# Where VectorE takes the attention's last three products out of PSUM, against the splits of the next segment's first operands

## The chip, the cores and the metric

The kernel runs on one core of a Trainium2 chip. The time is device microseconds of one execution, the median of several runs. The profile is of one execution, and its times are microseconds from the start of its span.

## The reference

The block computes a linear attention and multiplies it with a gated feed-forward network, with a residual:

```
xn = layernorm(x)                          # x: 2048 x 1024, fp32
q, k, v = split(xn @ wqkv)                 # 32 heads of 32
o = (phi(q) @ (phi(k)^T v)) / (phi(q) . sum(phi(k)) + 1e-6)
s = o @ wo                                 # the attention's output, 2048 x 1024
h = silu(xn @ w1) * (xn @ w3)              # 2048 x 3584
g = silu(h @ w2)                           # 2048 x 1024
out = x + s * g
```

## The kernel before

**Products.** Every large matrix product is done as a seven-product scheme on 2 x 2 blocks: `PRODUCTS = ["B11", "T2", "T3", "T1", "B21", "T4", "B22"]` names the right operands in the order of use, and `PARTNER` gives the left operand of each (A11, S2, S3, S1, A12, A22, S4). Each fp32 operand is split into two halves of the type fp32r, and each product of two 128 x 128 (by 512) tiles takes three matmuls: high x high (L103), high x low (L104), low x high (L105).

**Splits.** `split` (L91) makes the high half by a ScalarE cast (L95) and the low half by a VectorE subtraction (L96), which it returns. A raw operand comes by a DMA from SP's queue (L1286 for left operands, L1304 for right ones).

**The last two stages** are built from the class `Segment`. The first segment, `attention`, multiplies the scaled queries by the merged weights and gives s; after it come the feed-forward segments `layers`, which multiply h by w2 in pieces of 4 and 6 rows of 128. The first of them, `layers[0]` (two half rows, `nk` = 2), is the "second layer" of the change: the layer of operands that follows the attention. Each segment runs over `NG` = 8 blocks of 256 tokens. `right(k)` splits the seven right operands of half row k, `operands(m)` the seven left operands of block m, and `tokens(m, ...)` runs the products of block m and takes them out of PSUM.

**A block of the attention.** `tokens` uses four PSUM banks: ba (B11, then B21), bb (T2), bc (T3, then T4), bd (T1, then B22). The last three products end in c11 (a copy from ba, L1255), c21 (bc plus u) and c12 (bd plus u; both by `take`, L1199), all on VectorE. `end` then stores each c tile by a DMA from POOL's queue (L1328). The c tiles come from `small`, six buffers, which hold raw right operands of `layers[0]` too (T3 and T1 of half row 1 are loaded there ahead; B21, T4 and B22 follow as buffers come free).

**The first block of a segment** takes all seven banks at once (tiles named B11B, T2B and so on) and runs over k outside and over the products inside. The other blocks use four banks aB to dB.

**The change of segments.** Behind `run(attention, ...)` the pools of the attention's operands are closed and new ones are laid over them: `px` for the left operands (10 places of one buffer, and six raw buffers `pr`), `pw` for the right operands of half rows 1 and on. A new tile waits for the old tiles that it overlaps. Half row 0 of the right operands has been split during the attention (`first_weights`).

**Order.** Each engine works its queue strictly in the order in which it was laid down. A planner orders the queues by a simulated timeline, with the order in the code as priority. `with tc.issue_after(i)` adds an edge without a semaphore: what the block issues on the engine of instruction i comes behind i in that engine's queue. Before the change no such edge stands between the attention's evictions and the splits of `layers[0]`.

The names in the profile: `s<-as` is c11's copy, `s<-cs,us` and `s<-ds,us` the takes of c21 and c12, `XA11B<-rA11B` the split of the left operand A11 of a feed-forward segment, `B<-rB11B` and `T<-rT2B` those of right operands.

Of the kernel before, what the change touches and what calls it, by code (L numbers as in the profile page):

```python
# [22 lines left out]
def tile_linear_attention_times_swiglu(  # L23
# [27 lines left out]
    def bank(name):  # L51
        return ps.tile([P, C], F32, tag="bank", name=name)
# [38 lines left out]
    def split(pair, src, bias=None):  # L91

        hi, lo = pair[:, 0], pair[:, 1]
        if bias is None:
            nc.scalar.copy(out=hi, in_=src)  # L95
            return nc.vector.tensor_sub(out=lo, in0=src, in1=hi.bitcast(F32))  # L96
        nc.scalar.activation(hi, src, AF.Identity, bias=bias)
        return nc.vector.scalar_tensor_tensor(lo, src, bias, hi.bitcast(F32), op0=ALU.add, op1=ALU.subtract)
# [19 lines left out]
    def small(name):  # L118
        return pc.tile([P, C], F32, tag="c", name=name)
# [290 lines left out]
    class Operands:  # L410
# [35 lines left out]
        def place(self, n):  # L446
            self.B[n] = pb.tile([P, 2, ND // 2, P], FR, tag="b", name=f"{n}{self.name}")
            return self.B[n], self.b[n]
# [80 lines left out]
    def catch_up(*marks):  # L529

        for e in later:
            e[0] -= 1
        if later and later[0][0] <= 0:
            with ExitStack() as behind:
                for m in marks[-1:]:
                    behind.enter_context(tc.issue_after(m.ins))
                later.pop(0)[1]()
        elif jobs:
            job, in_order = jobs[0]
            with ExitStack() as behind:  # L540
                for m in marks + (tuple(fetched) if in_order else ()):
                    behind.enter_context(tc.issue_after(m.ins))
                if next(job, None) is None:
                    jobs.pop(0)
# [574 lines left out]
    for h in range(NH):  # L1119
        order = [(part, pair) for part in (1, 0) for pair in range(ND // 2)]  # L1120
        if h:
            order = [(part, pair) for pair in range(ND // 2) for part in (1, 0)]
        some = [Operands(wqkv, part * D + pair * 2 * P, f"{'qk'[part]}{h}_{pair}_", h == 0 and part == 1,
                         h and part == 0 and pair == 0)
                for part, pair in order]
# [17 lines left out]
    NG = S // GT  # L1143
    PARTNER = {"B11": "A11", "T2": "S2", "B21": "A12", "T3": "S3", "T1": "S1", "T4": "A22", "B22": "S4"}
    class Segment:


        def __init__(self, name, nk, first, last, place, right, left, acc, end=None):
            self.last, self.U = last, {}
            self.name, self.nk, self.first = name, nk, first  # L1150
            self.place, self.right_of, self.left_of, self.acc, self.end = place, right, left, acc, end
            self.Y, self.X = {}, {}

        def right(self, k, some=range(7)):

            for i in some:
                n = PRODUCTS[i]
                raw = self.right_of(n, i, k)
                self.Y[n, k] = self.place(n, i, k)
                split(self.Y[n, k], raw)  # L1160

        def operands(self, m):

            self.X[m] = {}
            if not self.first:

                self.U[m] = pe.tile([P, C], F32, tag="u", name=f"u{self.name}_{m}")
                nc.sync.dma_start(out=self.U[m], in_=u_d[m])
            for n, src in self.left_of(m):
                place = left_place if px else pb.tile  # L1170
                self.X[m][n] = place([P, 2, self.nk, P], FR, tag="b", name=f"X{n}{self.name}_{m}")
                split(self.X[m][n], src)

        def product(self, b, X, n, ks, start=True):
            for k in ks:
# [3 lines left out]
        def tokens(self, m, outer, between):  # L1179
            name = f"{self.name}_{m}"  # L1180
            X = self.X[m]
            c11, c12, c21, c22 = (self.acc(m, t, n) for t in range(2) for n in range(2))
            u = pe.tile([P, C], F32, tag="u", name=f"u{name}") if self.first else self.U[m]
            ks = range(self.nk)
            V, G = nc.vector, nc.gpsimd

            def end(t, n):
                if self.end:
                    self.end(m, t, n, ((c11, c12), (c21, c22))[t][n])

            def more(c, src):
                return V.tensor_add(out=c, in0=src, in1=c)  # L1192

            def take(c, src):

                if not self.first:
                    return more(c, src)
                if self.last:
                    return V.tensor_add(out=c, in0=src, in1=u)  # L1199
                return nc.scalar.copy(out=c, in_=src)  # L1200

            def close(e, c):

                if self.last and not self.first:
                    e.tensor_add(out=c, in0=c, in1=u)

            def keep():
                if not self.last:
                    G.dma_start(out=u_d[m], in_=u)  # L1209

            if outer:
                b = {n: bank(f"{n}{name}") for n in PRODUCTS}
                for k in ks:
                    for n in PRODUCTS:
                        self.product(b[n], X, n, [k])
                    between(k)
                if self.first:
                    nc.scalar.copy(out=u, in_=b["B11"])
                    V.tensor_add(out=c11, in0=b["B21"], in1=u)
                else:  # L1220
                    more(u, b["B11"])
                    more(c11, b["B11"])
                    more(c11, b["B21"])
                more(u, b["T2"])
                keep()
                take(c22, b["T3"])
                take(c21, b["T3"])
                more(c22, b["T1"])
                take(c12, b["T1"])
                more(c21, b["T4"])  # L1230
                more(c12, b["B22"])
                for c in (c22, c21, c12):
                    close(G, c)
                for t in range(2):
                    for n in range(2):
                        end(t, n)
            else:
                ba, bb, bc, bd = (bank(f"{n}{name}") for n in "abcd")
                self.product(ba, X, "B11", ks)
                copied = nc.scalar.copy(out=u, in_=ba) if self.first else more(u, ba)  # L1240
                catch_up(copied)
                self.product(bb, X, "T2", ks)
                added = more(u, bb)
                keep()
                catch_up(copied, added)
                self.product(bc, X, "T3", ks)
                added = take(c22, bc)
                catch_up(copied, added)
                self.product(bd, X, "T1", ks)
                added = more(c22, bd)  # L1250
                close(V, c22)
                end(1, 1)
                catch_up(copied, added)
                self.product(ba, X, "B21", ks, False)
                added = V.tensor_copy(c11, ba) if self.first else more(c11, ba)  # L1255
                end(0, 0)
                catch_up(copied, added)
                self.product(bc, X, "T4", ks, False)
                added = take(c21, bc)
                close(V, c21)  # L1260
                end(1, 0)
                close(G, c12)
                catch_up(copied, added)
                self.product(bd, X, "B22", ks, False)
                take(c12, bd)
                end(0, 1)

    loads, px = [], []
    turns = cycle([8, 0, 2, 1, 6, 9, 4, 3, 7, 5])
# [36 lines left out]
    def second_weights(i, n, k):  # L1306
        if (i, n, k) not in asked:
            ask(i, n, k, small)
        return asked[i, n, k]
# [95 lines left out]
    def attention_place(n, i, k):  # L1405
# [3 lines left out]
    attention = Segment("s", ND // 2, True, True, attention_place,  # L1409
                        attention_right, queries, lambda m, t, n: small(f"s{m}_{t}{n}"), store_s)  # L1410
# [8 lines left out]
    def layer_place(n, i, k):  # L1419
# [3 lines left out]
    layers = [Segment(f"B{i}", (f1 - f0) // 2, i == 0, i == len(FB) - 1, layer_place,  # L1423
                      lambda n, _, k, i=i: second_weights(i, n, k),
                      lambda m, i=i: hiddens(i, m), lambda m, t, n: acc[m][:, t, n],
                      finish if i == len(FB) - 1 else None)
              for i, (f0, f1) in enumerate(FB)]
# [9 lines left out]
    for i in range(10):  # L1437
        px[0].tile([P, 2, 3, P], FR, tag=f"b{i}", bufs=1, name=f"px{i}")
    ctx.enter_context(tc.tile_pool(name="pad", bufs=1, side="right")).tile([P, 2 * P], F32, name="pad")
    layers[0].operands(0)  # L1440
    pw.append(ctx.enter_context(tc.tile_pool(name="pw", bufs=1, side="right", reuse_waits="tile")))
    for k in range(1, layers[0].nk):
        layers[0].right(k)
    acc.append(pw0.tile([P, 2, 2, C], F32, tag="acc0", name="acc0"))
    acc.extend(pw[0].tile([P, 2, 2, C], F32, tag=f"acc{m}", name=f"acc{m}") for m in range(1, NG))
    for i, seg in enumerate(layers):
# [24 lines left out]
```

## Time and profile before

| | |
|---|---|
| median of three runs | 2317.89 us (2317.59 to 2320.45) |
| profiled execution | 2321.2 us, its span 2319.4 us |
| TensorE matmul busy | 2288.1 us, 99% |
| VectorE busy | 1762.9 us, 76% |
| ScalarE busy | 924.3 us, 40% |
| DMA | 478.69 MB, 206 GB/s in the mean |
| granted TensorE clock | 1.00 |

In a row of the timeline stand the start, the duration, the engine, the line, the operation, output<-inputs with their shapes, the count, and in brackets the idle time of the engine before the row and what ended it. A row of waits gives who waited for whom, the sum in us, how often, and the longest. In the table by stretches each engine's busy time stands with the number of its instructions, then the granted clock, the share of the DMA engines that was busy and GB/s.

### The profile page before, as it was taken

What the parts mean: (1) busy time and instruction counts of PE and PEld (TensorE: products, weight loads), DVE (VectorE), ACT (ScalarE), POOL (GpSimd) and SP (SyncE); (2) the same over time, 40 slices, a digit from 0 to 9 for tenths busy, and PEclk for the clock granted to TensorE, in tenths of its full rate; (3) what the DMA queues carried; (4) which work ended last, traced back from release to release, by engine and by line L of the source; (5) the groups of instructions that cost most, each with busy time, mean ns of one, the idle gap of its engine ahead of it and who ended that gap; (6) DMA issues with size and microseconds to landing.
All of it is one profiled execution on the core that took longest, in us unless ns stands there. A gap on an engine that the chain in (4) does not pass through costs nothing.

```text
span 2319.4 us, 31734 instructions
## 1 busy us (share of the span) xinstructions
PE 2288.1 (99%) x10752; PEld 1875.1 (81%) x10752; DVE 1762.9 (76%) x2843; ACT 924.3 (40%) x1644; POOL 658.6 (28%) x821
## 2 busy tenths in 40 slices
PE   7999999999999999999999999999999999999998
PEld 5888888888888887778888888888787888888877
DVE  8987888788776775567867788888655666767698
ACT  6555443433332555433333423234324624242433
POOL 2220524286754211001424344442210000000033
PEclk9999999999999999999999999999999999999999
DMA  6555556576659656875756666765755655766588
GB/s 241 163 186 177 186 164 200 163 240 209 214 181 322 222 177 216 271 260 187 227 187 186 191 205 205 215 205 175 234 175 187 190 180 175 233 201 184 181 264 274
DMA packets 353827, 478.69 MB, mean 206 GB/s; under 512 B 24209, under 2 KB 262801, under 8 KB 353553
## 3 DMA queue, kind: packets, MB, share of 16 engines
q1 hardware_dynamic: 316096, 357.11, 48.9%
q0 software_dynamic: 37568, 119.57, 15.9%
q8 instruction: 84, 1.38, 0.3%
q14 instruction: 79, 0.64, 0.1%
HBM read 305.66 MB, written 174.59 MB: 207 GB/s over the span
## 4 chain that ended last, share of the span: by engine, by line
PE 46%; DVE 3%; DMA 2%; issue 1%; POOL 1%; ACT 1%; SPq 0%; DVEq 0%; ACTq 0%; POOLq 0%
PE cB L103 1%; PE cB L105 1%; PE cB L104 1%; PE dB L104 1%; PE dB L105 1%; PE dB L103 1%; PE aB L104 1%; PE aB L105 1%; PE aB L103 1%; PE bB L105 1%; PE bB L104 1%; PE bB L103 1%; DMA rA22B<-h_d 1%; PE cs L103 1%; PE cs L104 1%
## 5 line engine op out<-in xcount | busy, mean ns | idle before, releaser
L883 POOL DMA_DIRECT2D h_d<-sg x112 | 82.6, 738 | 288.5 <-DVE sg L879 250.6
L1209 POOL DMA_DIRECT2D u_d<-uB x32 | 17.3, 541 | 405.7 <-DVE uB L1192 386.6
L96 DVE TENSOR_TENSOR xy<-xy,xy 128x512 fp32r<-128x512 f32 x112 | 72.8, 687 | 64.4 <-ACT xy L95 64.3
L95 ACT CAST xy<-xy 128x512 fp32r<-128x512 f32 x112 | 64.9, 620 | 102.1 <-PE g L105 58.8
L104 PE MATMUL g<-xy,xy 128*128 128x512 f32 x224 | 87.6, 391 | 0.2 <-DVE xy L96 0.2
L105 PE MATMUL g<-xy,xy 128*128 128x512 f32 x224 | 87.1, 390 | 0.0
L103 PE MATMUL g<-xy,xy 128*128 128x512 f32 x224 | 82.6, 398 | 0.2 <-ACT xy L95 0.2
L648 POOL DMA_DIRECT2D y_d<-y x48 | 34.6, 721 | 128.6 <-ACT y L672 75.2
L1192 DVE TENSOR_TENSOR acc<-cB,acc 128x512 f32<-128x512 f32 x50 | 34.5, 691 | 45.0 <-PE cB L105 45.0
L1192 DVE TENSOR_TENSOR acc<-dB,acc 128x512 f32<-128x512 f32 x56 | 38.7, 690 | 33.5 <-PE dB L105 33.4
L865 POOL TENSOR_TENSOR hs<-sg 128x256 f32<-128x256 f32 x56 | 59.7, 1066 | 0.0
L863 POOL TENSOR_TENSOR hs<-hs,sg 128x256 f32<-128x256 f32 x56 | 58.8, 1049 | 0.1
L103 PEld LDWEIGHTS g<-xy,xy 128*128 128x128 f32 x224 | 41.8, 188 | 14.6 <-issue 3.7
L866 POOL TENSOR_TENSOR hs<-sg,hs 128x256 f32<-128x256 f32 x56 | 51.7, 922 | 1.6
L1328 POOL DMA_DIRECT2D s_d<-s x32 | 17.3, 541 | 119.1 <-DVE s L1192 71.2
L1027 POOL DMA_DIRECT2D qs_d<-qd x32 | 18.1, 564 | 115.9 <-DVE qd L1023 95.8
L862 POOL TENSOR_TENSOR hs<-sg,sg 128x256 f32<-128x256 f32 x56 | 49.8, 889 | 1.2
L104 PEld LDWEIGHTS g<-xy,xy 128*128 128x128 f32 x224 | 42.1, 188 | 9.7 <-issue 0.8
L105 PEld LDWEIGHTS g<-xy,xy 128*128 128x128 f32 x224 | 42.0, 188 | 8.8
L891 POOL DMA_DIRECT2D h_d<-hs x60 | 46.4, 774 | 3.9 <-POOL hs L866 2.4
L804 POOL DMA_DIRECT2D pq_d<-pq x32 | 17.5, 548 | 97.5 <-DVE pq L638 97.3
L1028 POOL DMA_DIRECT2D qs_d<-qd x32 | 26.9, 840 | 48.3 <-DVE qd L866 38.2
(5331 smaller groups left out, 8245.2 us busy)
## 6 DMA issues: line engine op xcount, KB each, us to landing
h_d<-hs POOLq DMA_DIRECT2D x60, 256.0 KB, 3.1
h_d<-sg POOLq DMA_DIRECT2D x56, 256.0 KB, 4.0
w<-in_B_w SPq DMA_DIRECT2D x56, 256.0 KB
wt_d<-w SPq DMA_DIRECT2D x28, 512.0 KB
xy<-x_d SPq DMA_DIRECT2D x28, 512.0 KB
xy<-y_d SPq DMA_DIRECT2D x28, 512.0 KB
h_d<-hs SPq DMA_DIRECT2D x52, 256.0 KB
y_d<-y POOLq DMA_DIRECT2D x48, 256.0 KB, 3.1
```

The source lines that it names most:

```text
L95: nc.scalar.copy(out=hi, in_=src)
L96: return nc.vector.tensor_sub(out=lo, in0=src, in1=hi.bitcast(F32))
L103: nc.tensor.matmul(acc, lhsT=wh, rhs=ah, start=start, stop=False, skip_group_check=True)
L104: nc.tensor.matmul(acc, lhsT=wh, rhs=al, start=False, stop=False, skip_group_check=True)
L105: return nc.tensor.matmul(acc, lhsT=wl, rhs=ah, start=False, stop=stop, skip_group_check=True)
L862: e.tensor_add(out=s1, in0=a21, in1=a22)
L863: e.tensor_sub(out=s2, in0=s1, in1=a11)
L865: e.tensor_sub(out=s3, in0=a11, in1=a21)
L866: e.tensor_sub(out=s4, in0=a12, in1=s2)
L883: nc.gpsimd.dma_start(out=h_d[i][2 * h + c][:, 2 * n:4 * n + 2, k], in_=src)
L891: queue.dma_start(out=h_d[i][2 * h + c][:, 6 + 4 * e:10 + 4 * e, k], in_=o[e].rearrange("p (e s) -> p e s", s=P))
L1192: return V.tensor_add(out=c, in0=src, in1=c)
```

## The change

In the attention's last block the last three products are issued as before, but their evictions are handed over as a generator, `self.late`, and run later, in the code behind `layers[0].operands(0)`. The function `late` runs one step of it with an edge behind some of the splits that `made` has collected (the VectorE subtractions). `made.pop()` drops the split of S4, so the first step (c11's copy) comes behind the low halves of A11, S2, S3, S1 and A12; the second (c11's store, c21) and the third (c21's store, c12) behind those of A22 and of B11, T2, T3 and T1 of half row 1; the fourth stores c12. B21, T4 and B22 of half row 1 come in the code after that. `close` does nothing in this segment.

```diff
@@ class Segment
+            self.late, self.made = None, []
...
-                split(self.Y[n, k], raw)
+                self.made.append(split(self.Y[n, k], raw))
...
-                split(self.X[m][n], src)
+                self.made.append(split(self.X[m][n], src))
...
@@ tokens
-                self.product(ba, X, "B21", ks, False)
-                added = V.tensor_copy(c11, ba) if self.first else more(c11, ba)
-                end(0, 0)
-                catch_up(copied, added)
-                self.product(bc, X, "T4", ks, False)
-                added = take(c21, bc)
-                close(V, c21)
-                end(1, 0)
-                close(G, c12)
-                catch_up(copied, added)
-                self.product(bd, X, "B22", ks, False)
-                take(c12, bd)
-                end(0, 1)
+                def rest():
+                    yield V.tensor_copy(c11, ba) if self.first else more(c11, ba)
+                    end(0, 0)
+                    yield take(c21, bc)
+                    close(V, c21)
+                    end(1, 0)
+                    close(G, c12)
+                    yield take(c12, bd)
+                    end(0, 1)
+
+                taken = rest()
+                wait = self.first and self.last and m == NG - 1
+                for b, n in ((ba, "B21"), (bc, "T4"), (bd, "B22")):
+                    self.product(b, X, n, ks, False)
+                    if not wait:
+                        catch_up(copied, next(taken))
+                if wait:
+                    self.late = taken
+                else:
+                    next(taken, None)
...
+    def late(some):
+        with ExitStack() as behind:
+            for i in layers[0].made[some]:
+                behind.enter_context(tc.issue_after(i.ins))
+            next(attention.late, None)
+
     layers[0].operands(0)
+    layers[0].made.pop()
+    late(slice(-6, -1))
     pw.append(ctx.enter_context(tc.tile_pool(name="pw", ...)))
-    for k in range(1, layers[0].nk):
-        layers[0].right(k)
+    layers[0].right(1, range(4))
+    late(slice(-5, None))
+    late(slice(-5, None))
+    late(slice(-5, None))
+    layers[0].right(1, range(4, 7))
```

## The prediction

> **What bounds the kernel now.** I read the page first, for which engine is full.
>
> ```profile
> span 2319.4 us, 31734 instructions
> ...
> PE 2288.1 (99%) x10752; PEld 1875.1 (81%) x10752; DVE 1762.9 (76%) x2843; ACT 924.3 (40%) x1644; POOL 658.6 (28%) x821
> ```
>
> TensorE runs matmuls in all but 31.3 us of the span, and the change neither adds nor removes a matmul. Time can therefore come only out of those 31.3 us. The next view is what TensorE waited for from the attention's output projection (1640 us) to the end.
>
> ```profile
> PE cB L103 <- DVE acc L1192: 2.9, 1, 2.9
> PE B11B L105 <- DVE XA11B L96: 2.2, 1, 2.2
> ...
> PE cB L103 <- ACT acc L1200: 0.5, 1, 0.5
> PE dB L103 <- DVE acc L1192: 0.3, 1, 0.3
> ```
>
> The second row is the place of the change: the first matmuls of the first feed-forward segment ("the second layer" of the title) wait 2.2 us for VectorE's low half of the left operand A11. The table by stretches shows the surroundings.
>
> ```profile
> core 0: us, PE busy (x) PEld busy (x) DVE busy (x) ACT busy (x) POOL busy (x), PEclk, DMA share, GB/s
> ...
> 1756.00:1772.20 16.20, 16.20 (x73) 13.40 (x72) 3.46 (x5) 5.34 (x12) 1.62 (x3) 1.00 0.32 103
> 1772.20:1776.00 3.80, 1.63 (x8) 1.04 (x6) 3.59 (x7) 0.62 (x1) 0.54 (x1) 1.00 0.61 162
> 1776.00:1796.00 20.00, 20.00 (x89) 16.54 (x90) 17.26 (x37) 14.70 (x33) 1.08 (x2) 1.00 0.87 285
> ```
>
> For 16.2 us VectorE is busy 3.46 us, then it is full for 3.8 us while TensorE loses 3.80 - 1.63 = 2.17 us, and for the next 20 us it is still busy 86%. The DMA engines show the same: 32%, then 87%. Work that could have run early runs late. The VectorE timeline says why.
>
> ```profile
> 1764.25 0.69 DVE L1192 TENSOR_TENSOR s<-ds,s 128x512 f32<-128x512 f32 x1 [2.03 <-PE ds L105]
> 1766.97 0.69 DVE L1255 COPY s<-as 128x512 f32<-128x512 f32 x1 [2.03 <-PE as L105]
> 1769.69 0.69 DVE L1199 TENSOR_TENSOR s<-cs,us 128x512 f32<-128x512 f32 x1 [2.03 <-PE cs L105]
> 1772.41 0.69 DVE L1199 TENSOR_TENSOR s<-ds,us 128x512 f32<-128x512 f32 x1 [2.03 <-PE ds L105]
> 1773.02 0.68 DVE L96 TENSOR_TENSOR B<-rB11B,B 128x512 fp32r<-128x512 f32 x1
> 1773.61 0.69 DVE L96 TENSOR_TENSOR T<-rT2B,T 128x512 fp32r<-128x512 f32 x1
> ...
> 1775.42 0.42 DVE L96 TENSOR_TENSOR XA11B<-rA11B,XA11B 128x256 fp32r<-128x256 f32 x1
> 1775.75 0.42 DVE L96 TENSOR_TENSOR XS2B<-rS2B,XS2B 128x256 fp32r<-128x256 f32 x1
> ```
>
> The rows at 1766.97, 1769.69 and 1772.41 take c11, c21 and c12 out of PSUM; each stands idle 2.03 us until TensorE has finished its bank. The splits of the next segment follow behind the last of them, though ScalarE had made their high halves long before:
>
> ```profile
> 1762.21 0.62 ACT L95 CAST B<-rB11B 128x512 fp32r<-128x512 f32 x1 [5.53 <-PE ds L105]
> ...
> 1764.30 0.40 ACT L95 CAST XA11B<-rA11B 128x256 fp32r<-128x256 f32 x1
> ...
> 1765.53 0.40 ACT L95 CAST XA12B<-rA12B 128x256 fp32r<-128x256 f32 x1
> 1767.01 0.41 ACT L95 CAST XA22B<-rA22B 128x256 fp32r<-128x256 f32 x1 [1.08 <-issue]
> ...
> 1774.87 0.62 ACT L95 CAST T<-rT4B 128x512 fp32r<-128x512 f32 x1 [3.78 <-DMA rT4B<-wt_d]
> 1778.04 0.41 ACT L95 CAST XS4B<-rS4B 128x256 fp32r<-128x256 f32 x1 [2.55 <-DMA rS4B<-h_d]
> ...
> 1778.96 0.62 ACT L95 CAST B<-rB22B 128x512 fp32r<-128x512 f32 x1
> ```
>
> A11's high half is there at 1764.70 and its low half is begun at 1775.42, 10.7 us later.
>
> **The change part by part.** No operation is added or taken away; three evictions, with the stores of c11, c21 and c12 that POOL issues behind them, are placed later in VectorE's queue, and 9 splits come ahead of them: the left operands A11, S2, S3, S1, A12 before c11's copy, and A22 with the second-row halves of B11, T2, T3, T1 before c21 and c12.
>
> *VectorE.* Its own durations stay. Starts of wide splits are 1773.61 - 1773.02 = 0.59 us apart (0.60 from here on), of narrow ones 1775.75 - 1775.42 = 0.33 us (0.34). From the end of c22's add, 1764.25 + 0.69 = 1764.94, I take the worse order, wide ones first as they stand now: 4 x 0.60 + 5 x 0.34 = 4.1 us, so A11's low half is done near 1764.9 + 2.4 + 0.4 = 1767.7 and all nine near 1769.0. c11's copy (ready at 1766.97) then runs at 1769.0 to 1769.7, A22 (high half at 1767.42) at 1769.7 to 1770.1, c21 (ready at 1769.69) to 1770.8, and c12 is on time at 1772.41. So c11 comes 2.0 us later than now, c21 0.4 us, c12 not at all.
>
> *TensorE.* The rows of the stall:
>
> ```profile
> 1772.21 0.39 PE L103 MATMUL B11B<-B,XA11B 128*128 128x512 f32 x1
> ...
> 1773.34 0.39 PE L104 MATMUL T3B<-T,XS3B 128*128 128x512 f32 x1
> 1775.90 0.50 PE L105 MATMUL B11B<-B,XA11B 128*128 128x512 f32 x1 [2.17 <-DVE XA11B L96]
> ...
> 1784.19 0.39 PE L103 MATMUL aB<-B,XA11B 128*128 128x512 f32 x1
> ```
>
> Six matmuls go out from 1772.21 to 1773.34, (1773.34 - 1772.21) / 5 = 0.226 us apart, and the seventh, the first that needs a low half, is held. In the new order that half is there at 1767.7 and the matmul can be wanted at 1772.66 at the earliest in the code's order of products, 5 us of cover. Minus 2.17 us. If the cover went, that is what comes back.
>
> *What is late next.* Raw buffers and store slots set the loads behind. Rows of POOL and of SP's queue:
>
> ```profile
> 1767.96 0.54 POOL L1328 DMA_DIRECT2D s_d<-s  x1 [2.18 <-DVE s L1255]
> ```
>
> ```profile
> 1771.15 0.32 SPq L1304 DMA_DIRECT2D rT4B<-wt_d  x1
> 1775.87 0.32 SPq L1286 DMA_DIRECT2D rS4B<-h_d  x1
> 1776.31 0.36 SPq L1304 DMA_DIRECT2D rB22B<-in_B_w  x1
> ```
>
> rS4B starts 0.03 us after A11's low half ends (1775.42 + 0.42), whose raw buffer it takes; rT4B starts 1771.15 - 1767.96 = 3.19 us after c11's store is issued. After the change that store goes out at 1770.0 instead, which is c11's delay of 2.0 us handed to POOL and to SP. Unless T4 takes a slot that an earlier split frees, it is loaded at 1773.2, with rS4B behind it at 1773.6 and rB22B after c21's store (1771.1 + 3.2), at 1774.3. From issue to cast these took 3.72, 2.17 and 2.65 us, so their casts come at 1776.9, 1775.8 and 1777.0, against 1774.87, 1778.04 and 1778.96 now. In the code's order of products (seven of the first half row, then seven of the second, three matmuls of 0.226 us each) TensorE wants S4 at 1772.2 + 18 x 0.226 = 1776.3 (ready 1776.2), T4's second half at 1772.2 + 36 x 0.226 = 1780.3 and B22's at 1781.0. All arrive in time, S4 by a hair. Bounds of this term: 0 and, if rS4B is a further full load late (2.17 us), +2.2 us. I take 0, because TensorE's order is made to run other products first, as it does now (T3's second matmul stands ahead of B11's third).
>
> *The stretch behind.* 17.26 us of VectorE work and 87% DMA share between 1776 and 1796 get 4 us of splits and the loads that they release off their front. The 0.5 us wait of cB on ScalarE comes behind that stretch: between 0 and -0.5 us, and with no row that is nearer to one end I take half, -0.25.
>
> *PSUM.* c11's bank is held 2.0 us longer, c21's 0.4. Bounds: 0 where TensorE has another bank, +2.0 us where it stands for that one.
>
> ```profile
> 1753.37 0.69 DVE L1199 TENSOR_TENSOR s<-ds,us 128x512 f32<-128x512 f32 x1 [1.37 <-PE ds L105]
> 1758.88 0.69 DVE L1192 TENSOR_TENSOR us<-bs,us 128x512 f32<-128x512 f32 x1 [4.82 <-PE bs L105]
> ```
>
> The segment needs seven of eight banks. The last of the four of the block before was emptied at 1754.1, and a fifth, bb of this block, at 1759.6, so the sixth product wants c11's bank at 1772.2 + 15 x 0.226 = 1775.6, 5.9 us after the later copy. I take 0. The Trainium skill, page "PSUM — Partial Sum Buffer", section "Summary: rules for kernel authors", says to evacuate promptly since PSUM is small, which speaks against the change; by it the sum would lose the 2.0 us of c11's delay. No row of before shows that wait.
>
> *Sum:* -2.17 - 0.25 + 0 + 0 = -2.42 us against the profiled execution, whose span of 2319.4 becomes 2317.0. That execution took 2321.2 us with what lies around the span; the three timed runs have a median of 2317.89 us, 3.3 us below it, and no term above depends on that difference. So 2317.89 - 2.42 = 2315.5 us, 0.10% less. 0.2% (4.64 us) is about what a measurement of this kernel can tell from no change, so this counts as the same.
>
> **The rivals.** All work behind the edit is put in order by a planner, which sees the evictions at another place and may order everything after 1776 anew. The last segment is where that can count.
>
> ```profile
> 2240.00:2260.00 20.00, 17.12 (x76) 13.84 (x75) 17.40 (x30) 7.84 (x17) 4.95 (x6) 1.00 0.97 300
> 2260.00:2280.00 20.00, 20.00 (x89) 16.54 (x89) 20.00 (x36) 8.19 (x17) 9.15 (x9) 1.00 1.07 355
> ```
>
> ```profile
> 2239.06 7.18 DMA ss<-s_d
> ...
> 2253.56 0.50 PE cB L103
> ```
>
> *Faster by more.* The chain that ended last runs there through a 7.18 us fetch of s to the 2.9 us wait of cB, which is the TensorE time missing from the first of these rows (20.00 - 17.12). If the new order has this fetch out in time, 2.42 + 2.9 = 5.3 us go: 2312.6. For it: the wait is one chance collision. Against: right behind it VectorE is full (20.00 of 20.00), so what is late there is hardly made good.
>
> *Slower.* The same mechanism on the other side: the new order puts more of the fetches of the last segment behind loads of splits, VectorE's evictions start late, and each costs TensorE what this one does. From one extra on it eats the gain (-2.42 + 2.9 = +0.5), and it decides at three: -2.42 + 3 x 2.9 = +6.3 us, 2324.1. For it: a DMA share of 0.97 to 1.07 and that full VectorE, so nothing absorbs a late fetch. Against: TensorE waits there only once now.
>
> *The gap moves.* S4's load (2.2 us), or a bank, takes the place of the low half, or the splits do not run before 1772 at all because VectorE's new order holds them behind something not seen here. Between nothing and -0.25 us is left: 2317.8. For it: S4 is on time by 0.1 us only. Against: 10 us of free VectorE ahead of it.
>
> **How the numbers follow.** Forecast 0.43, faster by more 0.24, the gap moves 0.12, slower 0.21. The forecast's own range is 2314.9 (the waits of 2.2, 0.5 and 0.3 us all go) to 2315.7 (only the 2.17 us go); the unknown cost of S4's load is the third rival's. The rivals hold more than 2 in 10, so the range goes from 2312.0, under the faster case, to 2323.0, most of the way to the slower case's price. Faster by over 0.2%: 0.24; within: 0.43 + 0.12 = 0.55; slower: 0.21.
>
> **What would show it.** Right: in VectorE's timeline the low halves of A11 to A12 stand before c11's copy, between 1764.5 and 1769; c12's eviction stays at 1772.4; the row of B11B waiting for XA11B is gone from TensorE's waits; rS4B is issued before 1774; aB's first matmul comes near 1782.0 instead of 1784.19; last matmul 2.4 us earlier. Wrong: another wait of 1 us or more on TensorE between 1772 and 1784 (S4, T4 or a bank); or no such wait and still an end that is not earlier, when the last segment's waits tell whether the new order is to blame.

## The result and the profile after

The changed kernel took 2315.05 us (median, 2311.86 to 2318.11), the kernel before, timed beside it, 2318.47 us (2317.15 to 2325.39). The ratio is 0.9981, with a 95% interval from 0.9975 to 0.9987: 0.19% or 4.4 us less (3.0 to 5.8); the two medians lie 3.4 us apart. Forecast was 2315.5 us, 2.4 us less. The profiled execution after took 2314.25 us; that before, 2321.2 us.

The lines of the page after that answer to those shown of before:

```profile
span 2312.3 us, 31737 instructions
...
PE 2286.8 (99%) x10752; PEld 1875.7 (81%) x10752; DVE 1763.8 (76%) x2843; ACT 924.5 (40%) x1644; POOL 656.1 (28%) x821
```

The matmuls are the same number, and VectorE and ScalarE do the same work. Of TensorE's waits from 1640 us to the end, one row is left:

```profile
PE cB L103 <- DVE acc L1193: 2.0, 1, 2.0
```

The row of B11B waiting for XA11B is gone, and so is the row of cB waiting for ScalarE. This execution reaches the place 2.40 us earlier, with the segment's first matmul at 1769.81 instead of 1772.21 (before and after alike spread over some 3 us there), so the stretches are laid 2.40 us earlier too:

```profile
1753.60:1769.80 16.20, 16.20 (x73) 13.41 (x72) 7.69 (x15) 6.15 (x14) 1.63 (x3) 1.00 0.38 109
1769.80:1773.60 3.80, 3.80 (x18) 3.16 (x17) 1.96 (x4) 0.87 (x2) 0.54 (x1) 1.00 0.86 309
1773.60:1793.60 20.00, 20.00 (x90) 16.55 (x89) 16.91 (x34) 13.97 (x33) 1.63 (x3) 1.00 0.97 320
```

In the first stretch VectorE is now busy 7.69 us instead of 3.46; in the second TensorE is full (3.80 of 3.80, before 1.63), and the DMA engines show the same: 0.86 instead of 0.61. VectorE's timeline after:

```profile
1761.85 0.69 DVE L1193 TENSOR_TENSOR s<-ds,s 128x512 f32<-128x512 f32 x1 [2.03 <-PE ds L105]
1762.46 0.68 DVE L96 TENSOR_TENSOR B<-rB11B,B 128x512 fp32r<-128x512 f32 x1
...
1764.87 0.42 DVE L96 TENSOR_TENSOR XA11B<-rA11B,XA11B 128x256 fp32r<-128x256 f32 x1
...
1766.21 0.42 DVE L96 TENSOR_TENSOR XA12B<-rA12B,XA12B 128x256 fp32r<-128x256 f32 x1
1766.55 0.68 DVE L1256 COPY s<-as 128x512 f32<-128x512 f32 x1
1767.15 0.41 DVE L96 TENSOR_TENSOR XA22B<-rA22B,XA22B 128x256 fp32r<-128x256 f32 x1
1767.48 0.68 DVE L1200 TENSOR_TENSOR s<-cs,us 128x512 f32<-128x512 f32 x1
1770.01 0.69 DVE L1200 TENSOR_TENSOR s<-ds,us 128x512 f32<-128x512 f32 x1 [1.85 <-PE ds L105]
```

Nine splits stand ahead of c11's copy, without idle time between them, and c12 still goes out as soon as TensorE has its bank ready (1.85 us of idle time ahead of it). SP's queue shows what this set free:

```profile
1765.31 0.32 SPq L1294 DMA_DIRECT2D rS4B<-h_d  x1
...
1766.20 0.38 SPq L1312 DMA_DIRECT2D rB21B<-in_B_w  x1
1766.63 0.42 SPq L1312 DMA_DIRECT2D rT4B<-wt_d  x1
1767.11 0.42 SPq L1312 DMA_DIRECT2D rB22B<-in_B_w  x1
```

rS4B starts 0.02 us after A11's low half ends (1764.87 + 0.42), whose raw buffer it takes. The three right operands follow before c11 has been stored at all. TensorE after:

```profile
1769.81 0.39 PE L103 MATMUL B11B<-B,XA11B 128*128 128x512 f32 x1
...
1771.63 0.39 PE L105 MATMUL B11B<-B,XA11B 128*128 128x512 f32 x1
...
1776.16 0.39 PE L103 MATMUL B22B<-B,XS4B 128*128 128x512 f32 x1
...
1777.52 0.39 PE L103 MATMUL aB<-B,XA11B 128*128 128x512 f32 x1
```

No row of this stretch has a wait in brackets. S4's high half is used at 1776.16; its raw operand was issued 10.9 us before.

**Where the time went.** I cut each trace at the first matmul of every feed-forward segment. The second, third and fourth segment take 108.1, 114.2 and 114.2 us in every trace. From there on the work on every queue stands in the same order before and after; only some 70 us from the change on are ordered anew. So what the change does is in the first segment (the last segment is taken to the start of its last matmul):

| trace | first segment, us | wait for A11's low half | clock of 0.5 behind it | last segment, us | its wait of cB on VectorE |
|---|---|---|---|---|---|
| before | 67.22 | 2.17 | no | 136.17 | 2.88 |
| e1_before | 68.37 | 2.16 | yes | 136.59 | 2.31 |
| e5_before | 68.03 | 2.17 | yes | 134.03 | 1.29 |
| e11_before | 68.00 | 2.17 | yes | 138.18 | 3.92 |
| after | 63.92 | none | no | 134.78 | 1.98 |
| e2_after | 63.92 | none | no | 133.96 | 1.17 |
| e6_after | 63.92 | none | no | 136.72 | 2.49 |

Before: 67.9 us in the mean of four; after: 63.92 three times. The difference of 4.0 us is 0.17% of the kernel, and the ratios measured were 0.9981 and, repeated, 0.9983. The last segment varies by as much from one execution to the next on both sides (134.03 to 138.18 us before, 133.96 to 136.72 after); it is not counted as part of the change's effect.

### The profile page after: what moved, and what is told of

Read it like the earlier page. It is cut to its first block, busy times and chain, and to the rows that moved or that the text cites. A ratio compares the mean times of both kernels' runs of the same rounds, so it can differ in the third digit from the quotient of the medians.

```text
span 2312.3 us, 31737 instructions
## 1 busy us (share of the span) xinstructions
PE 2286.8 (99%) x10752; PEld 1875.7 (81%) x10752; DVE 1763.8 (76%) x2843; ACT 924.5 (40%) x1644; POOL 656.1 (28%) x821
## 4 chain that ended last, share of the span: by engine, by line
PE 83%; issue 6%; DVE 4%; DMA 3%; POOL 2%; ACT 0%; SPq 0%; DVEq 0%; POOLq 0%; ACTq 0%
PE g L103 2%; PE g L104 2%; PE g L105 2%; PE cB L103 2%; PE cB L104 2%; PE dB L104 2%; PE dB L105 2%; PE cB L105 2%; PE dB L103 2%; PE aB L104 2%; PE aB L105 1%; PE aB L103 1%; PE bB L105 1%; PE bB L104 1%; PE bB L103 1%
```

## The experiments

**Repeats, with no edit.** Four executions of the two kernels again, the first of each pair timed too.

> The kernel before, once more, for a second trace. Theory A (the boundary alone): the change is worth the 2.2 us wait on A11's low half and the 0.5 us wait behind it, 2.7 us in all, and whatever else differs between the two traces (1.4 us in the attention, 0.3 and 0.9 us in the last segment) changes from run to run. Then this trace shows the 2.2 and the 0.5 us wait again, and other waits elsewhere than the first trace. Theory B (the boundary and the last segment): the last segment waits less because everything arrives there earlier. Then this trace shows 2.9 us on cB and 0.3 us on dB again, within 0.3 us. Time: the same as before within 0.1%.

> The changed kernel, once more, for a second trace. Both theories: no wait of TensorE between 1750 and 1850 us, time 0.13 to 0.25% below before. Theory A: the last segment's wait on cB is anywhere between 1 and 4 us. Theory B: it is again 2.0 us, within 0.3 us.

> The kernel before, a third trace. Three readings so far: behind a wait of TensorE of 2.2 us or more the granted clock fell to 0.50 for about 3.4 us in some traces and not in others (behind the 2.16 us wait of e1_before yes, behind the 2.17 us of the first trace no). Theory A (the clock follows the wait by chance): the boundary wait is 2.2 us again, with or without a clock of 0.50 behind it; where it falls, about 8 matmuls take 0.43 us instead of 0.23, 1.6 us more. Theory B (the last segment differs): its wait on cB is between 2.3 and 2.9 us again.

> The changed kernel, a third trace. Theory A: no wait between 1750 and 1850 us, and no clock under 1 there. Theory B: the last segment's wait on cB is between 1.2 and 2.0 us again; if that difference to before is chance it falls outside.

Before against itself: 1.0001 [0.9992, 1.0009]. After: 2315.64 us, 0.9983 [0.9975, 0.9992]. Single times: 2317.28 (before) and 2319.16 (after), the wrong way round: one execution each tells nothing here. The gain is there again in the repeated times, and the wait for A11's low half is in each trace of before and in none of after. The last segment's wait of cB on VectorE was 1.29 to 3.92 us before and 1.17 to 2.49 us after, so theory B, by which it would come back within 0.3 us, does not hold. The trace of e1_before shows more than the first one had. TensorE's rows and then its stretches of one microsecond (the third figure from the right is the granted clock):

```profile
1773.49 0.50 PE L105 MATMUL B11B<-B,XA11B 128*128 128x512 f32 x1 [2.16 <-DVE XA11B L96]
...
1774.62 0.63 PE L105 MATMUL T2B<-T,XS2B 128*128 128x512 f32 x1
1775.05 0.63 PE L103 MATMUL T2B<-T,XS2B 128*128 128x512 f32 x1
...
1777.96 0.39 PE L104 MATMUL T3B<-T,XS3B 128*128 128x512 f32 x1
```

```profile
1774.00:1775.00 1.00, 1.00 (x4) 0.75 (x4) 1.00 (x4) 0.00 (x0) 0.00 (x0) 0.72 0.45 122
1775.00:1776.00 1.00, 1.00 (x4) 0.77 (x3) 1.00 (x3) 0.51 (x2) 0.00 (x0) 0.50 0.89 280
1776.00:1777.00 1.00, 1.00 (x4) 0.81 (x3) 0.66 (x2) 0.63 (x2) 0.00 (x0) 0.50 0.96 273
1777.00:1778.00 1.00, 1.00 (x4) 0.78 (x4) 0.60 (x1) 0.67 (x2) 0.00 (x0) 0.58 0.74 199
```

Behind the wait the granted clock is at 0.50 for about 3.4 us (0.56 us of the first slice, two whole ones and 0.84 us of the last), and matmuls start 0.43 us apart instead of 0.227. Eight of them cost 8 x 0.2 = 1.6 us, which is no idle time and stands in no row of waits. Once more the kernel before, to see how often that comes:

> The kernel before once more, for its trace alone: a third repeat of the wait of about 2.17 us on A11's low half. Of the three traces so far two show a granted clock of 0.5 in the 3.4 us behind the wait and one does not. Theory (whether the clock falls is decided by chance at each execution): one or the other, with the first segment at 68.0 to 68.4 us where it falls and near 67.2 us where it doesn't. Rival (the low clock is set by something else of the run): the first segment's length doesn't follow the clock.

It came: first segment 68.00 us, 2322.89 us in one execution. So three of these four traces have it.

**e3_c12_only: only c12 waits for the splits.** c11 and c21 are evicted where they were before.

```diff
-                    if not wait:
+                    if not wait or n != "B22":
                         catch_up(copied, next(taken))
...
     layers[0].made.pop()
-    late(slice(-6, -1))
...
     late(slice(-5, None))
     late(slice(-5, None))
-    late(slice(-5, None))
```

> Only the last of the three evictions, c12, comes behind the splits; c11 and c21 are taken out where before has them. VectorE is then free for the splits 2.7 us sooner than in before (behind c21 instead of c12): A11's low half ends 2.7 us sooner, 0.4 us before TensorE wants it. If the 2.2 us wait on that half is all that counts: the wait is gone and the time is as with the whole change, 0.1 to 0.2% below before. If what counts as well is that the loads and splits behind start 8 us sooner, most of that is lost here and part of the 0.5 us wait near 1800 stays: 0.05 to 0.12% below before.

2318.2 us, 0.9994 [0.9985, 1.0003]; first segment 66.17 us. VectorE, SP's queue and the one wait of TensorE in the segment:

```profile
1772.49 0.42 DVE L96 TENSOR_TENSOR XA11B<-rA11B,XA11B 128x256 fp32r<-128x256 f32 x1
```

```profile
1772.94 0.32 SPq L1294 DMA_DIRECT2D rS4B<-h_d  x1
```

```profile
1793.38 0.50 PE L103 MATMUL cB<-T,XA22B 128*128 128x512 f32 x1 [1.48 <-ACT acc L1201]
```

The first matmul is at 1772.00, A11's low half is done at 1772.91, and TensorE runs eight high products before it needs it: the wait at the change of segments is gone. Yet 2.25 us of the change's 4 us are missing. S4 is issued 0.94 us behind the segment's first matmul here, and 4.50 us ahead of it in the changed kernel (1765.31 against 1769.81). A wait comes back 21 us on, on ScalarE; with the longer step behind it, it is 1.75 us of the loss (steps of 1.87 and 0.34 us for two of 0.227), and four steps of 0.29 to 0.39 us ahead of it are 0.4 more. cB still holds the product T3, which ScalarE has to take out before T4's can begin, and ScalarE's queue stands for a load:

```profile
1791.92 0.62 ACT L95 CAST T<-rT4B 128x512 fp32r<-128x512 f32 x1 [1.70 <-DMA rT4B<-wt_d]
1792.75 0.58 ACT L1201 COPY acc<-cB 128x512 f32<-128x512 f32 x1
```

So about half of the gain is kept only when the loads behind the low half start early too. That this one load is late because S4 and those behind it started late is argued: the queues of this variant are also ordered anew.

**e4_all_last: all three evictions behind all seven second-row splits.**

```diff
     layers[0].made.pop()
-    late(slice(-6, -1))
...
     layers[0].right(1, range(4))
-    late(slice(-5, None))
...
     layers[0].right(1, range(4, 7))
+    late(slice(-8, None))
+    late(slice(-8, None))
+    late(slice(-8, None))
+    late(slice(-8, None))
```

> All three evictions come behind every split of the second half row too (B21, T4 and B22 as well), so c11's bank is held some 6 us longer than in before instead of none. If the segment has banks enough until its sixth product: no wait of TensorE on c11, c21 or c12, and the time of the whole change within 0.05%. If prompt evacuation counts: B21B or T4B waits 1 to 4 us for the bank, and the time is that of before or above it. Part of this would be the low halves of the left operands, which now stand behind the load of B22 (about 1770.5 in the time of before): up to 1 us of wait on A11.

2318.18 us, 0.9993 [0.9983, 1.0004]; first segment 66.76 us. VectorE's rows and TensorE's waits:

```profile
1768.88 0.69 DVE L96 TENSOR_TENSOR B<-rB21B,B 128x512 fp32r<-128x512 f32 x1 [3.67 <-ACT B L95]
...
1770.69 0.42 DVE L96 TENSOR_TENSOR XA11B<-rA11B,XA11B 128x256 fp32r<-128x256 f32 x1
...
1772.70 0.69 DVE L1256 COPY s<-as 128x512 f32<-128x512 f32 x1
```

```profile
PE cB L103 <- ACT acc L1201: 1.1, 1, 1.1
PE dB L103 <- ACT acc L1201: 0.9, 1, 0.9
```

c11 leaves its bank 2.45 us after the segment's first matmul (1770.25), against 3.26 us ahead of it in the changed kernel, 5.7 us later. No row shows TensorE waiting for a bank that VectorE had still to empty. What costs is the order: VectorE stands 3.67 us for the cast of B21, with A11's split behind it, so S4 is issued only at 1771.14, and two waits on ScalarE come back (1.2 and 1.4 of the 2.8 us lost, by the steps). The test does not reach the point where a bank is wanted: by the prediction's count it is the sixth product that wants c11's, T4 here; T4 begins 6.0 us after the segment's first matmul, and c11's copy has ended 3.1 us after it.

**e7_longer_stall: the wait made longer.** In the kernel before, a memset and sixteen additions on a scratch tile stand in VectorE's queue between c12 and the splits.

```diff
+    with tc.issue_after(attention.tail.ins):
+        nc.vector.memset(pad, 0.0)
+        for _ in range(16):
+            more_work = nc.vector.tensor_add(out=pad, in0=pad, in1=pad)
+    with tc.issue_after(more_work.ins):
+        layers[0].operands(0)
```

> Before, with a memset and 16 additions of 128x256 on scratch (about 0.3 + 16 x 0.34 = 5.7 us) in VectorE's queue between c12's eviction and the splits, and the low halves of the left operands next. TensorE's wait on A11's low half becomes 1773.1 + 5.7 + 0.4 - 1773.6 = 5.6 us instead of 2.2. If a wait here goes through to the end one for one: +3.4 us against before. If the granted clock falls behind every wait of this length: +3.4 us and about 0.8 us more, half of the 1.6 us that a low clock costs, since the wait of before has it sometimes: +4.2 us, 0.18%. If later slack takes it up: under +1.5 us.

2327.47 us, 1.0033 [1.0021, 1.0044], 7.7 us more; first segment 73.92 us. The wait became longer than meant, since a wide split that waited for its cast came in between the additions:

```profile
1782.16 0.79 PE L105 MATMUL B11B<-B,XA11B 128*128 128x512 f32 x1 [7.29 <-DVE XA11B L96]
...
1786.59 0.63 PE L105 MATMUL T4B<-T,XA22B 128*128 128x512 f32 x1
```

The wait is 5.12 us longer than before's 2.17. Against the 67.22 us without a lowered clock the segment is 6.7 us longer. The standstill and the step behind it cost 7.8 us (7.68 and 0.59 us for two steps of 0.227) instead of 2.44; eleven steps at the low clock cost 2.2 us; and the later wait of cB on ScalarE, 0.82 us in before, is gone: 5.38 + 2.17 - 0.82 = 6.73. Nothing behind this place makes the wait good.

**e9_kept_busy: the same stall, TensorE busy in it.** Thirty matmuls whose product is not read stand behind the attention's last one.

```diff
+    y, idle = layers[0].Y["B11", 0], bank("idle")
+    with tc.issue_after(attention.mm.ins):
+        for i in range(30):
+            nc.tensor.matmul(idle, lhsT=y[:, 0, :P], rhs=y[:, 0], start=True, stop=True, skip_group_check=True)
```

> The kernel with the longer stall (seventeen operations ahead of the splits), plus thirty matmuls of 128x512 whose product nobody reads, queued on TensorE right behind attention's last matmul, so that they run in the stretch in which that kernel's TensorE stood still for 7.29 us. At 0.227 us apart they fill 6.8 us. Theory (the low granted clock behind a wait is brought on by the standstill): the wait that is left is about 0.5 us, no slice behind it shows a clock of 0.5, and the first segment, counted from the block's first matmul, costs the same as there in standing time but without about ten matmuls at 0.43 instead of 0.227 us: about 2 us less, so 2325.5 us against the 2327.5 of the longer stall. Rival (the low clock comes from something else at this place, such as the burst of splits and casts on the other engines): the clock falls to 0.5 here too, and the time stays at 2327.5 us.

2324.3 us, 1.0019 [1.0010, 1.0029]. The stretches of e7_longer_stall:

```profile
1775.00:1782.00 7.00, 0.00 (x0) 0.00 (x0) 5.94 (x14) 1.85 (x3) 0.00 (x0) 0.65 0.29 83
...
1783.00:1784.00 1.00, 1.00 (x3) 0.74 (x3) 1.00 (x4) 0.04 (x1) 0.00 (x0) 0.50 0.68 197
1784.00:1785.00 1.00, 1.00 (x4) 0.77 (x3) 1.00 (x3) 0.69 (x2) 0.00 (x0) 0.50 0.80 265
```

and of e9_kept_busy:

```profile
1775.00:1782.00 7.00, 7.00 (x32) 5.59 (x32) 6.76 (x17) 1.65 (x3) 0.00 (x0) 1.00 0.39 113
...
1783.00:1784.00 1.00, 1.00 (x5) 0.82 (x6) 1.00 (x3) 0.52 (x2) 0.00 (x0) 1.00 0.78 239
1784.00:1785.00 1.00, 1.00 (x6) 0.82 (x5) 1.00 (x3) 0.88 (x3) 0.00 (x0) 1.00 0.69 153
```

With TensorE busy the clock stays at 1.00, though VectorE is just as full and the DMA engines are no quieter. It is the standstill that lowers it; the last section shows the same in all fourteen traces. From the attention's last matmul to the second segment this kernel takes 73.36 us and the other 74.14: the 2.2 us of clock are saved, but three new waits on ScalarE (0.93, 0.25 and 0.17 us of idle time) cost, with the longer steps behind them, 2.2 us again; what is left is that the thirty matmuls take 6.8 us and the standstill 7.8. The intervals of the two ratios overlap, so the times alone would not tell.

**The last segment.** Its wait of cB on VectorE comes in seven of the seven traces in the table. Three kernels tried it. In e8_close_pool, the closing addition of c22 goes from VectorE to GpSimd.

```diff
-                close(V, c22)
+                close(G if m < NG - 1 else V, c22)
```

> The changed kernel, with the last addition to c22 in the last segment (seven of 0.68 us on VectorE, blocks 0 to 6) given to POOL, which has c12's already. If VectorE's full load there is what makes cB wait, the wait of 1.2 to 2.9 us goes, with the low clock that sometimes follows: 1.5 to 3 us less than the changed kernel. If the wait comes from the fetches of s, it stays; and if POOL (1.3 to 2.7 us for one) is late with c22, the end comes up to 2 us later.

2316.87 us, 0.9987 [0.9978, 0.9996]: no better than the changed kernel. Two waits, 0.94 and 1.28 us, are there. In the changed kernel's trace, VectorE's rows and GpSimd's rows at the same time point the other way:

```profile
2213.69 1.78 DVE L1364 TENSOR_TENSOR acc<-acc,ss 128x512 f32<-128x512 f32 x1
2215.39 0.68 DVE L1193 TENSOR_TENSOR acc<-cB,acc 128x512 f32<-128x512 f32 x1
```

```profile
2213.38 1.54 POOL L1206 TENSOR_TENSOR acc<-acc,uB 128x512 f32<-128x512 f32 x1 [2.76 <-DVE acc L1193]
```

VectorE's product with the fetched s (L1364), of two SBUF operands, takes 1.78 us here, beside an addition of GpSimd, where most others take 0.68; it ends 0.55 us after GpSimd's. An addition that takes as long, 0.37 us behind the start of one on GpSimd, stands ahead of the wait of cB, which ends at 2246.50 in this trace; from it to the eviction at 2245.77 that frees the bank VectorE is not idle:

```profile
2241.46 1.77 DVE L1366 TENSOR_TENSOR acc<-acc,xs 128x512 f32<-128x512 f32 x1
2245.77 0.68 DVE L1193 TENSOR_TENSOR acc<-cB,acc 128x512 f32<-128x512 f32 x1
```

So e10_close_vector is the changed kernel, and e12_vector_only the kernel before, with c12's closing addition on VectorE:

```diff
-                    close(G, c12)
+                    close(V, c12)
```

> The changed kernel with the closing addition of c12 in the last segment's blocks on VectorE instead of GpSimd (the arithmetic is the same). In the changed kernel's trace an addition of VectorE took 1.78 us instead of 0.68 where GpSimd was in the middle of one of its ten closing additions (1.86 us each by the mean), and TensorE waits 2.0 us for cB there, on VectorE. Theory A (those waits are made by VectorE being slowed): VectorE takes on about 0.68 us for each addition and loses about 1.1 us less around each; the wait of 2.0 us shrinks to under 1 us and the last segment gets 1 to 2 us shorter: 2313.5 to 2314.5 us against the changed kernel's 2315.05. Rival B (the wait comes from the order in which VectorE does things, and one more operation in that order comes ahead of what TensorE needs): the wait grows by about 0.7 us a block, and the time is 2316 to 2318 us.

> The kernel before, with its three evictions where they were, and only the closing addition of c12 in the last segment's blocks on VectorE instead of GpSimd. With that addition on VectorE the changed kernel's last segment took 132.37 us from its first matmul to the end of the last, while the eleven traces with it on GpSimd took 133.96 to 138.18, and no wait for cB was left there. Theory A (that saving belongs to the last segment and is independent of the change under study): the last segment here is 132.4 us again without a wait over 1 us, the first stays at 67.2 to 68.4 us, and the time is 0.1 to 0.2% under the kernel before: a ratio of 0.998 to 0.999. Rival B (that run fell among the good ones by chance, as the wait there varied from 1.06 to 3.92 us from execution to execution): the wait of over 1 us is back, the last segment takes 134 to 138 us, and the time is that of the kernel before, a ratio of 1.000.

e10_close_vector: 2314.48 us, 0.9975 [0.9966, 0.9985] to the kernel before; first segment 63.92, last 132.37 us, and no wait of cB. e12_vector_only: 2318.16 us, 0.9995 [0.9986, 1.0004]; first segment 67.16, last 132.38 us, again without that wait, and with the wait of 2.16 us for A11 (without a lowered clock behind it this time). The twelve other traces, with the addition on GpSimd, had 133.96 to 138.18 us (135.7 in the mean), so theory A holds in the traces: the wait comes with those additions. In each of the twelve, four or five of VectorE's additions and products of two SBUF operands in this segment took over 0.9 us instead of 0.68 (3.9 to 5.1 us too much in all); in the two others one did (1.3 and 1.7 us). The edit also lets the planner order this segment anew, and how much of the saving is due to that is not shown. In the times it is not settled: the traces promise about 3.3 us, e12_vector_only's ratio says 1.2 us (between 3.2 less and 0.9 more), and the interval of e10_close_vector overlaps with that of the changed kernel. It has the lowest ratio of all kernels run, but that it beats the changed one is not shown.

## Why the prediction was right

*VectorE's order* went as worked out: low halves of A11 to A12 from 1764.87, c11's copy behind them, c21 late by little, c12 on time. Counted from the segment's first matmul, c11's copy came 1.98 us later than before (2.0 forecast), c21's 0.19 (0.4 forecast) and c12's not at all.

*The wait for A11's low half* is gone, but the term was short of its worth. The forecast took the idle time of the row, 2.17 us. Between the matmul ahead of the wait and the second behind it lie 2.56 + 0.33 us where two undisturbed steps of 0.227 us would do, 2.44 us in all: the two steps cost 0.27 us more than the idle time (called refilling below). Then comes the clock: at 0.50 behind the wait in three of four traces, 1.6 to 1.7 us each. This is where the step "Time can therefore come only out of those 31.3 us" fell short: matmuls at the low clock count as busy time. The profiled execution on which the forecast rested was the one without it, and nothing in that trace could show it.

*S4's load* cost nothing, as taken, but for another reason. The forecast had the raw right operands wait for c11's store and S4 come at 1773.6. They took buffers that the splits freed, S4 went first, at 1765.31 (1767.7 in the time of before), and aB's first matmul came 7.71 us after the segment's first, where 9.8 was forecast (1782.0 - 1772.2) and 11.98 stood before, since the order of TensorE's products was made anew as well. Against the segment's first matmul, S4's load went out 8.2 us earlier than before (4.50 us ahead of it instead of 3.66 behind), B22's 6.8 and T4's 2.1; only B21's, at 1767.66 before, was 0.9 us later.

*The stretch behind.* Half of a wait of 0.5 us was taken, -0.25 us. In the first trace that place cost 0.82 us with its refilling (matmuls 0.94 and 0.33 us apart at 1801.64 to 1802.91), in e1_before 0.34, in e5_before nothing; after, nothing. It was smaller in the traces where the clock had been low ahead of it, as if the other engines had time to catch up; that reason is argued. In the first trace, 2.44 + 0.82 = 3.26 of the 3.30 us of difference (67.22 - 63.92) are explained; in e1_before 2.44 + 1.7 + 0.34 = 4.48 of 4.45; in e5_before 2.44 + 1.7 = 4.14 of 4.11. So the gain is what the wait and what follows it cost; the early loads keep it from coming back elsewhere.

*PSUM.* No bank was waited for in the first segment, and e4_all_last, which holds c11 5.7 us longer still, shows no wait for a bank of the attention either; its two waits are for banks of the next segment that ScalarE empties late. The rule to evacuate promptly (the Trainium skill, "PSUM — Partial Sum Buffer", "Summary: rules for kernel authors") did not bind here.

*The rivals.* The last segment was not put in order anew, so neither the faster nor the slower of the first two could happen by its mechanism. That the gap moves was the live one: it did not in the changed kernel, but in e3_c12_only and e4_all_last it does, and gives back 2.25 and 2.84 of the 4.0 us. The gain is whole where S4's load goes out 4.50 us ahead of the segment's first matmul, and less than half of it is left where it goes out 0.94 and 0.89 us behind.

So the mechanism and the direction were right. That 2315.5 lies so near 2315.05 is in part luck: the gain forecast, 2.4 us, is below the interval measured (3.0 to 5.8), and the kernel before took 2318.47 us beside the changed one, not 2317.89. The measurement also told more than the 0.2% that the forecast gave it: its interval is 0.06% to either side. The mis-sized term is the first: -2.17 us should have been -2.44, and about one more microsecond in the mean for the clock (1.7 us in three of the four traces of before, and in none of e12_vector_only, which has the same wait).

## What to carry to other kernels

At a change of stages, look for an engine that stands in its queue before an eviction whose bank is not ready, with work behind it whose operands are; moving that work ahead can be worth more than the wait at the boundary (here 4.0 us for a wait of 2.17), and the buffers that it frees start the next loads. Price a stall of TensorE not by its idle row alone: add the longer steps behind it, and look at the granted clock behind it in more than one trace. And take the smallest delay of the evictions that lets the ready work through: in e4_all_last, which put three more splits ahead of them, the queue stood 3.67 us for one of these.

## What the runs showed of the hardware

*The clock falls behind short waits, when enough of one lies in one window.* Of the waits of TensorE of 2.1 us and more in the last 600 us of all fourteen traces, eight (2.16, 2.17, 2.17, 2.31, 2.49, 2.59, 3.92 and 7.29 us) had a clock of 0.50 in them or behind them, and four (2.16, 2.17, 2.88 and 3.33 us) had not; no shorter wait in these traces had. What tells them apart is in the clock records of the traces. From the first rise of the clock to the last matmul, every stretch of full clock in them is a whole number of times 3.413 us long (2300.58 us, 674 times, in the first trace of before; 474.45 us, 139 times, in e1_before), and a low stretch is 3.413 us, or three times that, 10.24 us, in e7_longer_stall. So the clock changes only at the marks of a grid of that pitch, whose place against the kernel is another in each execution.

I laid this grid over TensorE's idle time. Of all windows at full clock, over the whole of the fourteen traces, the eight with 2.03 us of idle time or more (2.03, 2.16, 2.17, 2.18, 2.26, 2.40, 2.59 and 3.41) were followed by a clock of 0.50, and none of those with 1.73 us or less was. The wait of 3.33 us in e3_c12_only was cut into 1.60 and 1.73 us, that of 2.17 us in the first trace of before into 0.71 and 1.46; the 2.16 us of e1_before fell into one window. An estimate from these figures: where the grid may lie anywhere, a wait of 2.17 us lowers the clock in 45% of the executions if it takes 2.03 us in one window, (3.41 + 2.17 - 2 x 2.03) / 3.41, and in 62% if it takes 1.73.

The Trainium skill, "TensorE: Matmul & The Clock Gate", section "What's actually happening", has the clock fall after an idle window of about 3.4 us and says that the window runs freely. The grid of 3.413 us agrees with that; that the whole window must be idle does not, as 2.03 us of it were enough.

*VectorE and GpSimd take turns.* A product of two SBUF operands took VectorE 1.78 us instead of 0.68 where it began 0.31 us after an addition of GpSimd (2213.69 against 2213.38). Further on in the same trace it goes the other way:

```profile
2257.75 2.74 POOL L1206 TENSOR_TENSOR acc<-acc,uB 128x512 f32<-128x512 f32 x1 [1.97 <-DVE uB L1193]
```

```profile
2258.05 1.28 DVE L1364 TENSOR_TENSOR acc<-acc,ss 128x512 f32<-128x512 f32 x2
2259.26 0.68 DVE L1193 TENSOR_TENSOR acc<-cB,acc 128x512 f32<-128x512 f32 x1
2259.86 1.04 DVE L96 TENSOR_TENSOR XA22B<-rA22B,XA22B 128x384 fp32r<-128x384 f32 x1
```

VectorE's two products of SBUF operands run at their usual length and GpSimd's addition takes 2.74 us instead of the 1.54 above; then the one with an operand in PSUM keeps its 0.68 us, and the split behind it, with two in SBUF, takes 1.04 instead of 0.54. The Trainium skill, "GPSIMD Engine Reference", section "Key points", says that the two engines share their SBUF interfaces and contend for instructions with two SBUF inputs. The rows agree.
